# Top-k attention with two expert layers: the scores' PSUM tile becomes two tiles with two copies, and the planner's table gets new numbers

## The chip, the cores and the metric

The kernel runs on one core of a Trainium2 chip. The core has five engines with a queue each: TensorE (PE, its weight loads shown as PEld), VectorE (DVE), ScalarE (ACT), GpSimd (POOL) and SyncE (SP, which here issues the DMAs). Every queue works in the order in which the program was written; an instruction that waits holds up all that stand behind it on its engine. The metric is the device time of the whole program in microseconds.

## What is computed

Four batches of 576 tokens with 8 heads of 64 columns go through attention in which each query keeps its 32 largest scores, then through a dense layer pair, then through eight experts of 288 tokens each, which a greedy rule assigns.

```python
scores = scale * np.matmul(q, k.transpose(0, 1, 3, 2))
kth = np.partition(scores, -top_k, axis=-1)[..., -top_k:-top_k + 1]
scores = np.where(scores >= kth, scores, -1000000000.0)
attn = np.exp(scores - np.max(scores, axis=-1, keepdims=True))
attn = attn / (np.sum(attn, axis=-1, keepdims=True) + 1e-09)
x = np.matmul(attn, v)                       # then tokens x (heads * 64)
h = x @ w_in
g = np.where(h >= 1, h, np.where(h <= -1, 0.0, (h + 1) ** 2 / 4))
x = g @ w_out
logits = x @ w_gate                          # greedy: best (token, expert) pairs first,
# each token once, each expert at most 288 tokens
h = np.maximum(x[mask] @ w1[e], 0.0)
out[mask] = h @ w2[e]
```

## The kernel before

There are two phases, and the order of the instructions in each is made by a small planner inside the program. Every operation is recorded (`_Recorder`, L213) with an estimated cost, and `Program.issue` (L166) lays the operations out with a list scheduler. Whenever an engine is free, it takes the ready operation with the smallest key. An operation is ready when its inputs are done and a hand-over time has passed (`_delay`, L128, from the tables `LAT`, `TO` and `SELF`, L57 to L59, with a factor `LATX` of 1.5 in the first phase). The keys come first from ranks that the code sets, and then from a pass that runs backward. Of eleven such rounds in the first phase (`ROUNDS`, L44) and twenty-one in the second the one with the earliest planned end is issued. The planner knows of an order between two operations only where one writes what the other reads or writes (L107). The framework that builds the program adds the semaphores to the instructions in the order that the planner gives.

The first phase does attention in steps. A step is one batch, one block of 128 query tokens (the fifth block has 64) and one pair of heads: 64 full steps with two heads one after the other, and 16 short ones. `scores` (L497) makes the two halves of a head's 576 scores as two groups of matmuls, in two banks of one PSUM tile `pS` (L287): half 0 in bank 0, half 1 in bank 1. ScalarE copies both halves with one instruction to an SBUF tile `s` (L527). Then VectorE makes the fold (L531): the larger of half 0, read from bank 0, and half 1, read from the copy, to a tile `f`; for some heads VectorE also makes the smaller of the two (L533), and for the others GpSimd derives it. `topk` (L544) runs four maxima of eight and three replacements on VectorE, a mask on ScalarE and GpSimd, and the exponential on ScalarE. `transposed` and `values` transpose the weights through PSUM (`pPT`, `pQ`) and multiply with v. When 256 tokens are complete, `ffn_block` (L694) runs the dense pair on them through the banks `pH` and `pX`, split in high and low parts (`gh`, `gl`, `whi`, `wl`). TensorE fills its time between the attention steps with this. In the first 140 us VectorE also decodes the 32 pieces of 64-bit weights (`decode`, L415; first operation `pH<-stage` or `pH<-s`, L426).

The second phase (`second_phase`, L843) finishes the last dense block, routes the tokens to one expert after the other (small VectorE operations with short matmuls between them, into `pQ`, `pPT` and `pS`), gathers each expert's 288 rows with indirect DMAs from GpSimd (L1245), runs the expert, and scatters its rows. Beside that, `look` (L1212) reads weight pieces again and ScalarE sums them (`size`); from all sums `totals` (L1221) makes a flag, which all engines read at the end (L1381) before a branch that is not taken here.

The lines that decide the order around the scores:

```python
pS = psum.tile([128, 2, 512], F32, name="pS")
T.matmul(pS[:, hf, o_:o_ + n], q_t[:, z, k, :], ks[k][:, c0:c0 + n], ...)
A.activation(s_sb[:, i, :].rearrange("p (a x) -> p a x", a=2), pS[:, :, :288], AF.Relu)
V.tensor_tensor(out=f[i][:, :HW], in0=pS[:, 0, :HW], in1=s_sb[:, i, HW:], op=ALU.max)
```

Of the kernel before, what the change touches and what calls it, by code (L numbers as in the profile page):

```python
# [9 lines left out]
F32 = mybir.dt.float32  # L10
# [38 lines left out]
LOW_ACT, CLIP_ACT, R_UK = (), (0,) * 9, {}  # L49


class Program:
# [26 lines left out]
    def _new(self, eng):  # L79
        op = {"eng": eng, "calls": [], "cost": 0.0, "lat": self.LAT[eng], "deps": set(), "rank": self.rank,  # L80
              "n": len(self.ops)}
        self.ops.append(op)
        return op

    @staticmethod
    def _span(ap):
# [16 lines left out]
        if t.space == bass.MemoryType.PSUM:  # L103
            return t.name, 0, 128, lo * size // 2048 * 2048, (hi * size // 2048 + 1) * 2048
        return t.name, p0, p1, lo * size, (hi + 1) * size

    def add(self, eng, call, cost, reads, writes, lat=None):  # L107
        op = self.grp or self._new(eng)
        op["calls"].append(call)
# [18 lines left out]
    def _delay(self, a, b):  # L128
        e, f = a["eng"], b["eng"]
        if e == "sync":  # L130
            return a["lat"]
        return self.SELF[e] if e == f else a["lat"] * self.latx + self.TO.get((e, f), 0)

    def _pass(self, key, heads, tails, clock):
# [7 lines left out]
        free = dict.fromkeys(engs, 0.0)  # L142
        soon = {e: [] for e in engs}
# [4 lines left out]
        while len(order) < len(ops):  # L148
# [9 lines left out]
            stop[n] = free[e] = t + (clock.run(t, cost) if clock and e == "tensor" else cost)  # L158
# [7 lines left out]
    def issue(self, rounds=0):  # L166
# [10 lines left out]
        for r in range(rounds + 1):  # L177
            stop, order, end = self._pass(key, heads, tails, _Clock(self.warm))
            if best is None or end < best[0]:
                best = end, order  # L180
            if r < rounds:
                back = self._pass([-x for x in stop], tails, heads, None)
                key = [-x for x in back[0]]
        for n in best[1]:
            for call in ops[n]["calls"]:
                call()
        self.ops, self.hist = [], {}

# [24 lines left out]
class _Recorder:  # L213
# [5 lines left out]
    def __getattr__(self, method):  # L219
        def rec(*args, **kw):  # L220
# [12 lines left out]
            lat = None  # L233
            if eng == "vector":
# [3 lines left out]
                if method == "tensor_scalar" and not inp:  # L238
# [12 lines left out]
            elif eng == "gpsimd":  # L251
                cost = 148 + 2.1 * n
# [3 lines left out]
            elif method == "transpose":  # L256
                cost = 109
            else:
                f32 = args[1].dtype == F32
                if args[1].dtype == F32R:  # L260
                    cost = 10 + 0.43 * n
                else:
                    cost = 2 * max(107, n * 2 / 2.4) + 1 if f32 else max(25 if _free(args[1]) == 128 else 45, n / 2.4 + 3)
                if f32 and args[1].shape[-1] <= 64:
                    cost *= 0.63
            fn = getattr(getattr(P.nc, eng), method)
            P.add(eng, lambda: fn(*args, **kw), cost, reads, writes, lat)  # L267
# [11 lines left out]
def kernel(ctx: ExitStack, tc: tile.TileContext, qm, qt, kT, vm, vt,  # L279
# [7 lines left out]
    pS = psum.tile([128, 2, 512], F32, name="pS")  # L287
# [84 lines left out]
    def first_phase(exact, actx):  # L372
# [124 lines left out]
        def scores(b, j, p, r, exact):  # L497
# [19 lines left out]
            for i in range(2 if full else 1):  # L517
                for hf in range(2):
# [3 lines left out]
                    with P.group():  # L522
                        for x, (k, o_, c0, n) in enumerate(parts):
                            for z in range(2):
                                T.matmul(pS[:, hf, o_:o_ + n], q_t[:, z, k, :], ks[k][:, c0:c0 + n],
                                         start=(x + z == 0), stop=(x == len(parts) - 1 and z == 1))
                A.activation(s_sb[:, i, :].rearrange("p (a x) -> p a x", a=2), pS[:, :, :288],  # L527
                             AF.Copy if exact else AF.Relu)
                if not exact:
                    f.append(t_f())  # L530
                    V.tensor_tensor(out=f[i][:, :HW], in0=pS[:, 0, :HW], in1=s_sb[:, i, HW:], op=ALU.max)  # L531
                    if fold_dve(b, j, p, i):
                        V.tensor_tensor(out=f[i][:, HW:], in0=pS[:, 0, :HW], in1=s_sb[:, i, HW:], op=ALU.min)  # L533
# [123 lines left out]
        def values(b, j, ps, r, made):  # L657
# [3 lines left out]
            accs = [pQ[:, 256 + 128 * n:384 + 128 * n] for n in range(2)]  # L661
# [155 lines left out]
        for b in range(B):  # L817
            for j in range(5):
                for p in range(NP):
# [3 lines left out]
                    values(b, j, (p,), at, made)  # L823
                    made = []
                    at += 1.0 if j < 4 else 0.6
                    if j == 4 and b + 1 < B:
                        P.rank = at + R_K
                        load_pair(b + 1, p)
                    if p == NP - 1 and (b, j) == (B - 1, 4):
# [3 lines left out]
                        ffn_end(k, [pS[:, t] for t in range(2)])  # L833
# [6 lines left out]
        P.issue(0 if exact else ROUNDS)  # L840


    def second_phase(exact, rctx):  # L843
# [55 lines left out]
        XT0 = [pH[0], pH[1], pS[:, 0, :], pX[0]]  # L899
# [555 lines left out]
```

## Time and profile before

| what | value |
|---|---|
| median of three runs | 1122.76 us (1122.61 to 1126.74) |
| the profiled execution, its own time | 1125.48 us |
| its span | 1123.7 us |
| TensorE busy in the span | 1043.9 us (93%) |
| VectorE busy | 913.1 us (81%) |
| ScalarE busy | 808.3 us (72%) |
| GpSimd busy | 699.4 us (62%) |
| granted TensorE clock, mean | 0.957 |

The span runs from the first to the last instruction of the profiled execution; 1.8 us of its own time lie outside. Busy time is the time in which an engine had at least one instruction under way. A matmul's end is modelled, and matmuls overlap, so a TensorE that is busy all the time may still lose some time between instructions. A line of a wait says which engine and tile waited, for which engine and tile, how long in total and how often. All recorded operations carry the line of the recorder, L267, so they are told apart by their tiles.

### The profile page before, as it was taken

Reading aid. Unit: us, or ns where it says so; the run is one execution under the profiler, and the core shown is the slowest. Engines: PE = TensorE matmul, PEld = TensorE weight load, DVE = VectorE, ACT = ScalarE, POOL = GpSimd, SP = SyncE. Lnnn points to the kernel's source line nnn. Section 1 sums busy time; section 2 is a strip of 40 time slices with the busy share of each in tenths; the row PEclk is TensorE's granted clock in tenths of the full one; section 3 lists DMA queues with packets and bytes.
Section 4 is the critical chain, followed back from the end, with each engine's and each line's share of the span. In section 5 each row is a group of like instructions: output and inputs, shape, how many; then the busy total and the mean of one; then the engine's idle time right before and its main releaser. Section 6 shows DMA issues by size and latency. Waiting matters only on the chain.

```text
span 1123.7 us, 24286 instructions
## 1 busy us (share of the span) xinstructions
PE 1043.9 (93%) x8376; PEld 940.6 (84%) x8376; DVE 913.1 (81%) x2638; ACT 808.3 (72%) x1899; POOL 699.4 (62%) x880
## 2 busy tenths in 40 slices
PE   2687799999999999999999999999998999999995
PEld 1566589888888888899988889898976999999994
DVE  7899999899999889988989999994248998775530
ACT  4677787888898888877888988875314666666652
POOL 6997988987887888757689788773211143223111
PEclk9966689999999999999999999999988999999998
DMA  9743432351221342221234221212227777787721
GB/s 260 234 146 122 146 129 79 111 160 58 85 77 62 97 151 93 72 92 65 81 100 134 90 76 51 85 60 65 97 74 234 265 273 237 236 262 253 264 97 44
DMA packets 65783, 149.35 MB, mean 133 GB/s; under 512 B 15472, under 2 KB 23920, under 8 KB 65648
## 3 DMA queue, kind: packets, MB, share of 16 engines
q1 hardware_dynamic: 62576, 138.25, 37.7%
q0 software_dynamic: 3072, 9.44, 2.6%
q8 instruction: 68, 1.11, 0.4%
q14 instruction: 67, 0.55, 0.2%
HBM read 133.50 MB, written 14.16 MB: 131 GB/s over the span
## 4 chain that ended last, share of the span: by engine, by line
PE 64%; DVE 14%; ACT 7%; issue 5%; POOL 4%; DMA 4%; SPq 0%; POOLq 0%; DVEq 0%; ACTq 0%
PE pH L267 23%; PE pX L267 23%; PE pQ L267 7%; PE pS L267 7%; DVE f L267 5%; DVE m L267 5%; PE pPT L267 4%; ACT s L267 3%; DVE stage L267 2%; POOL s L267 2%; POOL XB L267 1%; ACT f L267 1%; DMA s<-in_w_in_dram 1%; DVE pH L267 1%; POOL f L267 1%
## 5 line engine op out<-in xcount | busy, mean ns | idle before, releaser
L267 PE MATMUL pH<-XB,W 128*128 128x256 f32 (+1 forms) x2496 | 360.1, 291 | 0.8 <-DVE L L267 0.5
L267 PEld LDWEIGHTS pH<-XB,W 128*128 128x128 f32 x2496 | 327.8, 190 | 8.2 <-issue 2.7
L267 DVE MAX8 m<-f 128x8 f32<-128x288 f32 (+1 forms) x576 | 290.9, 525 | 6.7 <-POOL f L267 1.1
L267 POOL TENSOR_TENSOR s<-s,f 128x576 f32<-128x576 f32 x144 | 204.2, 1432 | 29.5 <-ACT f L267 28.4
L267 DVE MATCH_REPLACE8 f<-m,f 128x288 f32<-128x288 f32 x432 | 190.2, 442 | 0.2
L267 PE MATMUL pX<-W,XB 128*128 128x512 f32 x608 | 184.9, 412 | 0.0
L267 PE MATMUL pS<-XB 128*128 128x288 f32 (+2 forms) x672 | 143.0, 324 | 37.8 <-DVE f L267 16.0
L267 POOL TENSOR_TENSOR XB<-stage,XB 128x512 fp32r<-128x512 f32 (+1 forms) x96 | 127.3, 1326 | 62.4 <-ACT XB L267 47.6
L267 PEld LDWEIGHTS pS<-XB 128*128 128x128 f32 x672 | 106.3, 201 | 57.8 <-DVE f L267 20.0
L267 ACT ACTIVATE s<-s,sm 128x576 f32<-128x576 f32 x144 | 111.8, 777 | 22.1 <-POOL s L267 21.5
L267 PEld LDWEIGHTS pX<-W,XB 128*128 128x128 f32 x608 | 108.2, 192 | 18.0 <-issue 2.4
L267 PE MATMUL pX<-XB,W 128*128 128x288 f32 x768 | 113.7, 299 | 0.0
L267 ACT ACTIVATE s<-pS 128x576 f32<-128x576 f32 x144 | 92.9, 645 | 25.7 <-PE pS L267 23.8
L267 ACT ACTIVATE f<-s,t_all 128x576 f32<-128x576 f32 x144 | 107.9, 772 | 2.9
L267 DVE TENSOR_TENSOR f<-pS,s 128x288 f32<-128x288 f32 x198 | 85.7, 448 | 23.3 <-ACT s L267 10.5
L267 PEld LDWEIGHTS pX<-XB,W 128*128 128x128 f32 x768 | 104.4, 188 | 0.0
L1245 POOL DMA_INDIRECT xg<-dram_x,idx x24 | 34.0, 1417 | 113.0 <-DVE idx L267 55.3
L267 PE MATMUL pPT<-ident,s 128*128 128x128 f32 x576 | 92.9, 286 | 7.0 <-ACT s L267 6.9
L1339 POOL DMA_INDIRECT out_dram<-yo,idx x24 | 28.3, 1179 | 110.3 <-ACT yo L267 107.9
L267 ACT ACTIVATE s<-pPT 128x512 f32<-128x512 f32 x144 | 85.2, 592 | 9.6 <-PE pPT L267 9.2
L267 DVE TENSOR_TENSOR W<-raw,W 128x1024 fp32r<-128x1024 f32 x64 | 77.1, 1219 | 15.7 <-ACT W L267 15.7
L267 PE MATMUL pQ<-s,v 128*64 128x128 f32 (+1 forms) x1280 | 87.2, 282 | 2.3 <-ACT tr L267 2.3
(206 smaller groups left out, 1906.6 us busy)
## 6 DMA issues: line engine op xcount, KB each, us to landing
wl<-dram_wlo SPq DMA_DIRECT2D x64, 512.0 KB, 3.3
raw<-in_w_dram SPq DMA_DIRECT2D x64, 512.0 KB, 5.5
s<-in_w_in_dram SPq DMA_DIRECT2D x18, 512.0 KB, 4.4
s<-in_w_out_dram SPq DMA_DIRECT2D x18, 512.0 KB, 3.9
qr<-in_qm_dram SPq DMA_DIRECT2D x128, 64.0 KB, 2.2
stage<-in_w_in_dram SPq DMA_DIRECT2D x14, 512.0 KB, 4.1
stage<-in_w_out_dram SPq DMA_DIRECT2D x14, 512.0 KB, 3.3
stage<-in_kT_dram SPq DMA_DIRECT2D x48, 144.0 KB, 2.8
```

The source lines that it names most:

```text
L267: P.add(eng, lambda: fn(*args, **kw), cost, reads, writes, lat)
L1245: return nc.gpsimd.indirect_dma_start(out=xg[:, g, :], out_offset=None, in_=x2d[:, :], in_offset=bass.IndirectOffsetOnAxis(ap=idx[:, g:g + ...
L1339: st = nc.gpsimd.indirect_dma_start(out=out, out_offset=bass.IndirectOffsetOnAxis(ap=idx[:, g:g + 1], axis=0), in_=yo, in_offset=None)
```

## The change

The tile `pS` of two banks becomes two tiles of one bank, `pS[0]` and `pS[1]`. In `scores` the group of half 1 comes first, and after each group ScalarE copies that half alone, so a head has two copies of 128x288 in place of one of 128x576. The folds are as before; they read bank 0 and the copy of half 1.

The planner's numbers change. A hand-over now has its own number for each pair of engines, and the factor of 1.5 is no longer used. A change of the kind of matmul (plain, 64-column, transpose) has a price (`TURN`). Six costs are altered: VectorE's scalar operations that write PSUM, GpSimd's long operations, and four kinds of matmul. PSUM tiles are now taken as wholes by the planner, which is the same for tiles of one bank. A search over shaken keys (`SEEDS`) and a grouping of steps (`PAIRS`) are added and left at values that do nothing: no seeds, and one step at a time.

```diff
-    LAT = {"vector": 140, "scalar": 170, "gpsimd": 75, "tensor": 200, "sync": 0}
-    TO = {("tensor", "vector"): 90, ("scalar", "tensor"): 100, ("gpsimd", "tensor"): 100, ("vector", "tensor"): 60}
-    SELF = {"vector": 128, "gpsimd": 103, "scalar": 0, "tensor": 0}
+    LAT = {"vector": {"scalar": 112, "gpsimd": 160, "tensor": 137, "vector": 128, "sync": 210},
+           "scalar": {"vector": 142, "gpsimd": 187, "tensor": 165, "scalar": 130, "sync": 255},
+           "gpsimd": {"vector": 170, "scalar": 102, "tensor": 117, "gpsimd": 130, "sync": 112},
+           "tensor": {"vector": 205, "scalar": 200, "gpsimd": 205, "tensor": 0, "sync": 300}}
+    TURN = {(0, 1): 90, (2, 1): 93, (1, 0): 150, (1, 2): 150, (2, 0): -81}
...
-        return self.SELF[e] if e == f else a["lat"] * self.latx + self.TO.get((e, f), 0)
+        return a["lat"] if e == "sync" else self.LAT[e][f]
...
-                if method == "tensor_scalar" and not inp:
+                if method == "tensor_scalar" and not inp and not outp:
                     cost = 69 + 0.52 * n
...
-                cost = 148 + 2.1 * n
+                cost = 148 + 2.1 * n + (27 if n > 500 else 0)
...
-    pS = psum.tile([128, 2, 512], F32, name="pS")
+    pS = [psum.tile([128, 512], F32, name=f"pS{i}") for i in range(2)]
...
-                for hf in range(2):
+                for hf in (1, 0):
...
-                                T.matmul(pS[:, hf, o_:o_ + n], q_t[:, z, k, :], ks[k][:, c0:c0 + n],
+                                T.matmul(pS[hf][:, o_:o_ + n], q_t[:, z, k, :], ks[k][:, c0:c0 + n],
...
-                A.activation(s_sb[:, i, :].rearrange("p (a x) -> p a x", a=2), pS[:, :, :288],
-                             AF.Copy if exact else AF.Relu)
+                    A.activation(s_sb[:, i, HW * hf:HW * hf + HW], pS[hf][:, :HW], AF.Copy if exact else AF.Relu)
...
-                    V.tensor_tensor(out=f[i][:, :HW], in0=pS[:, 0, :HW], in1=s_sb[:, i, HW:], op=ALU.max)
+                    V.tensor_tensor(out=f[i][:, :HW], in0=pS[0][:, :HW], in1=s_sb[:, i, HW:], op=ALU.max)
...
-        P.issue(0 if exact else ROUNDS)
+        P.issue(0, ()) if exact else P.issue(ROUNDS, SEEDS)
```

What the change does to the order is seen in the queues. The first place is ScalarE in the middle of the first phase, at the 85th and 86th of the 144 heads; `pS` is the tile of two banks, `s` the copy, and in brackets stands whose semaphores the instruction waits for. Before:

```order
L267 ACTIVATE s_107<-pS 128x576 [waits PE_49]
L267 ACTIVATE f_132<-sm_136 128x128 [waits DVE_49]
L267 ACTIVATE stage<-stage,mhalf 128x512 [waits DVE_49]
L267 ACTIVATE s_105<-pPT 128x512 [waits PE_49]
L267 ACTIVATE s_107<-pS 128x576 [waits PE_49]
```

After, where `pS_67` is bank 1 and `pS_66` is bank 0:

```order
L304 ACTIVATE s_108<-pS_67 128x288 [waits PE_49]
L304 ACTIVATE s_108<-pS_66 128x288 [waits PE_49]
L304 ACTIVATE stage<-stage,mhalf 128x512 [waits DVE_49]
L304 ACTIVATE f_133<-sm_137 128x128 [waits DVE_49]
L304 ACTIVATE s_108<-pS_67 128x288 [waits PE_49]
L304 ACTIVATE s_106<-pPT 128x512 [waits PE_49]
L304 ACTIVATE t_all<-m_139 128x2 [waits DVE_49]
L304 ACTIVATE s_108<-pS_66 128x288 [waits DVE_49]
```

Each copy became two, the copy of bank 1 ahead of that of bank 0, and the second head's copies are apart, with other work between them; its copy of bank 0 waits for VectorE, which before no score copy here did. In the whole program 47 of the 144 copies of bank 0 wait for a fold, and of the 198 folds 81 wait for the copy of bank 0 and 39 for that of bank 1; the others wait for neither by themselves.

The second place is TensorE's queue at the first expert's gathered rows `xg`; `ident` is the identity for transposes, `I_0` belongs to the ranks of the tokens, `W`, `XB` with `pX` to the last dense block. Before:

```order
L267 LDWEIGHTS I_0_9487
L267 MATMUL pQ<-C_9477,I_0_9487 128x8
L267 LDWEIGHTS ones_f
L267 MATMUL pPT<-ge_9489,ones_f 128x8 [waits DVE_49]
L267 MATMUL pH_69<-ident,xg_9524 128x96 [waits DMASW0_49]
L267 MATMUL pH_69<-ident,xg_9524 128x96 [waits DMASW1_49]
```

After:

```order
L304 LDWEIGHTS I_0_9632
L304 MATMUL pQ<-C_9622,I_0_9632 128x8
L304 MATMUL pX_73<-W_96,XB 128x512 x4
L304 MATMUL pX_73<-W_97,XB 128x512
L304 LDWEIGHTS ones_f
L304 MATMUL pPT<-ge_9633,ones_f 128x8 [waits DVE_49]
L304 MATMUL pX_73<-W_97,XB 128x512 x3
L304 MATMUL pX_73<-W_98,XB 128x512 x4
L304 MATMUL pX_73<-W_99,XB 128x512 x4
L304 MATMUL pH_70<-ident,xg_9669 128x96 [waits DMASW0_49]
```

Twelve `pX` matmuls of the last dense block now stand behind the ranks and ahead of the transposes of `xg`, where none stood. Counted from the router's last matmul that the gather needs (`Bt`, `oh`), 23 matmuls into `pX` stand ahead of the transposes, where 15 stood.

The third place is the end of ScalarE's queue. `s` is the last expert's result on its way, `yo` its rows before they are scattered, `size` belongs to the look at the weights, and `TENSOR_LOAD flag` is the reading of the flag. Before:

```order
L267 ACTIVATE s_107<-pX_71 128x288 [waits PE_49]
L267 ACTIVATE size_9533,sizes<-s_106 128x512 [waits DMAHW6_49,Activation_49]
L267 ACTIVATE size_9533,sizes<-size_9533 128x512 [waits Activation_49]
L267 ACTIVATE s_107<-pX_72 128x288 [waits PE_49]
L267 ACTIVATE yo_9528<-pS 96x512 [waits DMASW2_49,PE_49]
L267 ACTIVATE yo_9526<-pX_71 96x512 [waits DMASW3_49,PE_49]
L267 ACTIVATE yo_9527<-pS 96x512 [waits DMASW4_49,PE_49]
L1381 TENSOR_LOAD flag [waits DVE_49]
```

After:

```order
L304 ACTIVATE size_9678,sizes<-size_9678 128x512 [waits Activation_49]
L304 ACTIVATE s_108<-pX_73 128x288 [waits PE_49]
L304 ACTIVATE yo_9673<-pS_66 96x512 [waits DMASW2_49,PE_49]
L304 ACTIVATE yo_9671<-pX_72 96x512 [waits DMASW3_49,PE_49]
L304 ACTIVATE yo_9672<-pS_66 96x512 [waits DMASW4_49,PE_49]
L304 ACTIVATE size_9678,sizes<-s_107 128x512 [waits DMAHW6_49,Activation_49]
L304 ACTIVATE size_9678,sizes<-size_9678 128x512 [waits Activation_49]
L1421 TENSOR_LOAD flag [waits DVE_49]
```

The last pair of `size` operations has moved behind the three `yo` copies, and with it the small operations on VectorE and TensorE that make the flag.

## Rows read from the trace of the kernel before

**Rows 1.** Busy time of the engines by stretch of the span (us).

```profile
core 0: us, PE busy (x) PEld busy (x) DVE busy (x) ACT busy (x) POOL busy (x), PEclk, DMA share, GB/s
0.00:28.00 28.00, 5.88 (x22) 4.84 (x23) 21.06 (x46) 11.25 (x19) 17.49 (x26) 1.00 0.95 260
28.00:140.00 112.00, 84.54 (x458) 67.09 (x456) 103.72 (x284) 81.09 (x196) 100.68 (x119) 0.71 0.49 163
140.00:756.00 616.00, 604.83 (x4931) 540.67 (x4932) 568.94 (x1716) 522.29 (x1281) 493.59 (x640) 0.99 0.28 91
...
868.00:1107.00 239.00, 238.68 (x2127) 233.93 (x2127) 160.53 (x403) 153.15 (x326) 57.88 (x64) 1.00 0.68 229
```

**Rows 2.** Groups by form, whole span: busy us, mean ns; idle before, its releasers.

```profile
L267 PE MATMUL pS<-XB 128*128 128x288 f32 x608 | 137.5, 331 | 37.8 <-DVE f L267 16.0 <-POOL XB L267 15.8 <-ACT s L267 3.3
...
L267 ACT ACTIVATE s<-pS 128x576 f32<-128x576 f32 x144 | 92.9, 645 | 25.7 <-PE pS L267 23.8 <-POOL f L267 1.0 <-POOL XB L267 0.2
...
L267 ACT ACTIVATE s<-pX 128x288 f32<-128x288 f32 x32 | 13.1, 408 | 28.5 <-PE pX L267 28.4
...
L267 DVE TENSOR_TENSOR f<-pS,s 128x288 f32<-128x288 f32 x198 | 85.7, 448 | 23.3 <-ACT s L267 10.5 <-PE pS L267 6.1 <-PE pQ L267 2.0
```

**Rows 3.** Waits, 140 to 756 us: who <- for whom: total us, times, longest.

```profile
PEld pS L267 <- DVE f L267: 7.3, 13, 1.2
PE pS L267 <- DVE f L267: 6.3, 11, 0.8
...
DVE f L267 <- ACT s L267: 8.9, 11, 1.6
...
ACT s L267 <- PE pS L267: 16.6, 24, 2.3
```

**Rows 4.** Waits of TensorE for the folds from 0 to 140 us.

```profile
PE pS L267 <- DVE f L267: 9.7, 8, 2.1
```

**Rows 5.** Timeline of score steps, ACT, PE, DVE: start, length, operation, [wait <- releaser].

```profile
402.47 0.63 ACT L267 ACTIVATE s<-pS 128x576 f32<-128x576 f32 x1
...
403.00 0.27 ACT L267 ACTIVATE s<-pQ 128x128 f32<-128x128 f32 x1
...
405.60 0.51 PE L267 MATMUL pS<-XB 128*128 128x288 f32 x2
...
406.35 0.63 ACT L267 ACTIVATE s<-pS 128x576 f32<-128x576 f32 x1
...
408.03 0.45 DVE L267 TENSOR_TENSOR f<-pS,s 128x288 f32<-128x288 f32 x1
...
408.62 0.51 PE L267 MATMUL pS<-XB 128*128 128x288 f32 x2 [0.84 <-DVE f L267]
```

**Rows 6.** Timeline of the first gather: TensorE, then GpSimd, then TensorE.

```profile
851.13 1.41 PE L267 MATMUL pX<-W,XB 128*128 128x512 f32 x5
...
854.93 0.71 PE L267 MATMUL pX<-W,XB 128*128 128x512 f32 x2
...
853.33 1.23 POOL L1245 DMA_INDIRECT xg<-dram_x,idx  x1 [28.17 <-DMA s<-in_w_in_dram]
...
859.74 0.55 PE L267 MATMUL pH<-ident,xg 96*128 96x96 f32 x2 [0.96 <-DMA xg<-dram_x,idx]
```

**Rows 7.** The tail: timelines of ACT and DVE, then the chain on POOL.

```profile
1104.93 0.65 ACT L267 ACTIVATE size<-s 128x512 f32<-128x512 f32 x1
...
1109.96 0.59 ACT L267 ACTIVATE yo<-pS 96x512 f32<-96x512 f32 x1 [0.25 <-PE pS L267]
...
1106.46 0.18 DVE L267 TENSOR_SCALAR sizes<-sizes 128x32 f32<-128x32 f32 x1 [0.57 <-ACT size L267]
...
1108.31 0.14 DVE L267 TENSOR_REDUCE flag<-flags 1x1 int32<-1x3 f32 x1
...
1111.65 0.03 POOLq L1381
...
1111.95 0.92 POOL out_dram L1339
```

More of the change, by code (lines that the diff above doesn't have):

```diff
@@ L103, in _span, with add @@
         if t.space == bass.MemoryType.PSUM:
-            return t.name, 0, 128, lo * size // 2048 * 2048, (hi * size // 2048 + 1) * 2048
+            return t.name, 0, 128, 0, 1 << 30
         return t.name, p0, p1, lo * size, (hi + 1) * size
-    def add(self, eng, call, cost, reads, writes, lat=None):
+    def add(self, eng, call, cost, reads, writes, lat=None, mode=0):
         op = self.grp or self._new(eng)
+        op["mode"] = mode
         op["calls"].append(call)
@@ L142, in _pass @@
         free = dict.fromkeys(engs, 0.0)
+        mode = 0
         soon = {e: [] for e in engs}
@@ L157, in _pass @@
             cost = ops[n]["cost"]
-            stop[n] = free[e] = t + (clock.run(t, cost) if clock and e == "tensor" else cost)
+            if clock and e == "tensor":
+                cost += self.TURN.get((mode, ops[n]["mode"]), 0)
+                mode = ops[n]["mode"]
+                cost = clock.run(t, cost)
+            stop[n] = free[e] = t + cost
             for m, gap in tails[n]:
@@ L176, in issue, with look @@
         key, best = [o["rank"] for o in ops], None
-        for r in range(rounds + 1):
+        def look(key):
+            nonlocal best
             stop, order, end = self._pass(key, heads, tails, _Clock(self.warm))
             if best is None or end < best[0]:
-                best = end, order
+                best = end, order, key
+            return stop
+        for r in range(rounds + 1):
+            stop = look(key)
             if r < rounds:
@@ L183, in issue @@
                 key = [-x for x in back[0]]
+        for seed in seeds:
+            look(_shaken(best[2], best[0], seed))
         for n in best[1]:
@@ L187, in issue, with _shaken, draw @@
         self.ops, self.hist = [], {}
+def _shaken(key, end, seed):
+    x = (seed * 2654435761 + 12345) % 4294967296
+    def draw():
+        nonlocal x
+        x = (x * 1664525 + 1013904223) % 4294967296
+        return x / 2147483648.0 - 1.0
+    size = SHAKE * 2.0 ** -(seed % 5)
+    if seed % 2 == 0:
+        return [k + size * draw() for k in key]
+    at = 0.5 * end * (draw() - 1.0)
+    return [k + 2.0 * size * draw() if abs(k - at) < 40000.0 else k for k in key]
 class _Clock:
@@ L237, in rec @@
                     cost += 64
-                if method == "tensor_scalar" and not inp:
+                outp = any(a.tensor.space == bass.MemoryType.PSUM for a in writes if hasattr(a.tensor, "space"))
+                if method == "tensor_scalar" and not inp and not outp:
                     cost = 69 + 0.52 * n
@@ L251, in rec @@
             elif eng == "gpsimd":
-                cost = 148 + 2.1 * n
+                cost = 148 + 2.1 * n + (27 if n > 500 else 0)
+                if n == S and writes[0].dtype == F32R:
+                    cost += 115
             elif eng == "sync":
@@ L660, in values @@
             w = 128 if full else 64
-            accs = [pQ[:, 256 + 128 * n:384 + 128 * n] for n in range(2)]
+            accs = [pQ[:, 256 + 128 * (x % 2):384 + 128 * (x % 2)] for x in ps]
             with P.group():
@@ L822, in first_phase @@
                     made.append(transposed(b, j, p, at, s_sb, rinv, wide))
-                    values(b, j, (p,), at, made)
-                    made = []
+                    done = len(made) == PAIRS
+                    if done:
+                        ps = tuple(range(p + 1 - PAIRS, p + 1))
+                        values(b, j, ps, at, made)
+                        made = []
                     at += 1.0 if j < 4 else 0.6
-                    if j == 4 and b + 1 < B:
+                    if done and j == 4 and b + 1 < B:
                         P.rank = at + R_K
-                        load_pair(b + 1, p)
+                        for x in ps:
+                            load_pair(b + 1, x)
                     if p == NP - 1 and (b, j) == (B - 1, 4):
@@ L832, in first_phase @@
                         k, P.rank = late.pop()
-                        ffn_end(k, [pS[:, t] for t in range(2)])
+                        ffn_end(k, pS)
                     if p == NP - 1:
@@ L1172, in route @@
             V.tensor_tensor_scan(sc, tk, tk, 0.0, op0=ALU.add, op1=ALU.bypass)
-            T.matmul(pS[:, 1, 8:9], tri, sc[:, NT - 1:NT], start=True, stop=True)
+            T.matmul(pS[1][:, 8:9], tri, sc[:, NT - 1:NT], start=True, stop=True)
             pos = rt([128, NT], F32, "pos")
-            V.scalar_tensor_tensor(out=pos, in0=sc, scalar=pS[:, 1, 8:9], in1=most, op0=ALU.add, op1=ALU.min)
+            V.scalar_tensor_tensor(out=pos, in0=sc, scalar=pS[1][:, 8:9], in1=most, op0=ALU.add, op1=ALU.min)
             places(ph, ei, pos)
```

39 lines of the change are left out of this document (21 added, 18 removed).

## The prediction

> **What bounds the kernel now.** I read the busy times by stretch first [rows 1]. The program has different limits in different stretches. Up to 28 us the DMA engines are busy 95% of the time and TensorE only 5.88 us. From 28 to 140 us VectorE is the limit: it is busy 103.72 of 112 us, because it decodes weights beside the top-k, while TensorE has 84.54 us of work at a mean granted clock of 0.71. From 140 to 756 us TensorE is the limit, with 604.83 of 616 us and a clock of 0.99, so only 11.2 us can be gained there by keeping it fed; VectorE has 47.1 us free, ScalarE 93.7 us. From 868 to 1107 us TensorE is busy 238.68 of 239 us, and no order of the other engines can shorten that. So the change can act in the first 140 us, in the 11.2 us, at the start of the experts, and at the end.
>
> Then I read what ends TensorE's waits in the middle [rows 3]. It waits for a fold before it may overwrite `pS`: 6.3 us in 11 waits, and its weight load, which stands just ahead of the matmul, 7.3 us in 13. ScalarE waits 16.6 us for TensorE's scores. The first two rows are the same stalls seen twice, so I count 6.3 us, over half of the 11.2. In the first 140 us the same wait costs 9.7 us in 8 cases [rows 4]. The timeline of a case [rows 5]: a copy runs from 406.35 for 0.63 us and is done at 406.98, but the fold starts only at 408.03, since VectorE has other work first; the next scores' matmuls wait 0.84 us for it and start at 408.62. The copy held nothing up there; the fold was late by itself.
>
> **Part 1, two copies in place of one.** A copy of 128x576 lasts 645 ns, one of 128x288 (from another PSUM tile) 408 ns [rows 2]. So 144 x (2 x 408 - 645) ns = 24.6 us more ScalarE time, at most; at the pace at which the next instruction starts, 0.53 us after the large copy [rows 5], it is less. All of it lies on ScalarE, which has 93.7 us free in the middle. Queued behind a longer copy are the weights' exponentials and the copies of `pPT`, for which TensorE waits. I take 0, with 3 us as the upper end: 24.6 x 11.2 / 93.7, as if the extra time reached TensorE in the proportion in which it has idle time left.
>
> **Part 2, what the halves release.** Now the half in bank 1 comes first and needs only its own copy to be overwritten; the half in bank 0 still waits for the fold. In a wait as in [rows 5] TensorE can do the bank-1 pair meanwhile: two matmuls take 0.51 us end to end and one lasts 0.331 [rows 2], so they follow each other by 0.18, and a pair is worth 0.36 us of a wait. With 11 waits that is 4.0 us. Bank 1's copy also starts a pair earlier and is 0.24 us shorter, so the fold's second source is there 0.6 us sooner; that helps 11 waits of VectorE worth 8.9 us [rows 3], but VectorE has time to spare here, so I give it, and the planner's numbers (hand-overs per pair of engines without the 1.5 factor), only 1 us more. Middle: **-5 us**, between 0 and -11.2.
>
> **Part 3, a wait that the code does not show.** In the changed order 81 of the 198 folds wait for the copy of bank 0, which they do not use, and 47 of the 144 copies of bank 0 wait for a fold: both read bank 0, and they are kept from doing it together. In the kernel before, one copy stood ahead of the fold anyway. The planner does not know of this order. The Trainium skill has the reason ("PSUM — Partial Sum Buffer", section "PSUM bank collisions raise a hardware error"): two different engines that access one bank and partition quadrant at the same time, two readers included, raise an error, so software must order them. By that rule the two copies cannot free the fold from bank 0's copy, so the 1 us that Part 2 gives the earlier fold goes, and the middle is -4.0 instead of -5, the sum 1116.7 instead of 1115.7; no row of the trace before shows two readers of one bank together, so it neither agrees nor differs. The price from rows: a fold held for a whole copy loses 0.408 us [rows 2], so 81 of them lose at most 33 us of VectorE time; a copy held for a fold loses at most 0.448, 47 of them 21 us of ScalarE time. Both fit in the 47.1 and 93.7 us free in the middle, and most folds will find the copy finished, as in [rows 5] where the fold came 1.05 us after it. I take 0 and keep a loss as a rival.
>
> **Part 4, the first 140 us.** Three things move: the first two loads are now those of k instead of a weight piece (first decode perhaps 1 us later, first scores earlier), the first seven folds stand up to thirteen places further ahead in VectorE's queue, and the costs of the decode are now planned near their real size. The 9.7 us of waits [rows 4] is what could go, worth 8 x 0.36 = 2.9 us by the reckoning of Part 2. VectorE has 8.3 us free between 28 and 140 us, which limits the rest. On the other side about a dozen of the first 24 folds (VectorE's first 300 instructions, of 330 in this stretch [rows 1]) wait for ScalarE: 12 x 0.408 = 4.9 us where VectorE is the limit. I take **-2 us**, between -8 and +5.
>
> **Part 5, the first gather.** In the changed order 23 matmuls of the last dense block stand between the router's last matmul for the gather and the expert's first transposes, where 15 stood. In the trace GpSimd starts the gather at 853.33, TensorE ends its `pX` work at 855.64 and starts the transposes at 859.74 [rows 6]. Eight more matmuls at (1.41 - 0.71) / 3 = 0.23 us each fill 1.9 us of that hole: **-1.9 us**, between 0 and -2.5.
>
> **Part 6, the end.** The last pair of `size` operations starts at 1104.93 [rows 7], inside time that nothing waits for. It now comes behind the last `yo` copy, which starts at 1109.96 and lasts 0.59. From the first `size` to the end of the flag's last operation (1108.31 + 0.14) it took 3.52 us, part of it while TensorE was still in its last `pX` work, which is then over; I take 2.9. From 1110.5, where the last `yo` copy lets ScalarE go on, the flag comes at 1113.4. GpSimd, the last engine to read it, did so at 1111.65. So **+1.8 us**, between 0 (if the last scatter, 1111.95 to 1112.87, decides the end instead) and +2.4.
>
> The second phase between these places keeps its work: 0, within 2 either way.
>
> **The sum** against the profiled execution's own 1125.48 us: 0 - 5 + 0 - 2 - 1.9 + 1.8 = -7.1, so 1118.4. That execution was 2.7 us above the median; I put the same -7.1 on the median 1122.76: **1115.7 us**, or -0.63%. A measurement of this kernel can tell about 0.5%, 5.6 us, from no change: faster means below 1117.1, slower above 1128.4.
>
> **Rivals.** *Nothing measurable.* The fold is late through VectorE's own queue, as [rows 5] says, and the fold still holds bank 0; then only the 4.0 us of Part 2 are real or less, the first 140 us give nothing, and Part 6 takes 1.8 back: 1122.8 - 4.0 - 1.9 + 1.8 + 0 = 1118.7, and up to 1125 where the new order loses as much as it gains elsewhere; I put it at 1121. For it speaks that only 11.2 us are to be had; against it that the waits are the largest of TensorE's in the middle. In this case the change would do what its code says and not what it is worth, since fold and copy of bank 0 are still in sequence.
>
> *Slower by Part 3.* The place is the fold in VectorE's queue. Each fold that waits for the bank-0 copy also holds up the maxima behind it, then the mask, the transposes and TensorE. Up to 33 us would use VectorE's 47.1 us; it decides once the waits in a stretch are larger than VectorE's spare time there, and it is worst before 140 us where only 8.3 are spare. If a quarter of 33 reaches TensorE, that is +8.3 and nothing of Parts 2 and 4 is left: 1122.8 + 8.3 - 1.9 + 1.8 = 1131. For it speaks that the planner prices none of this; against it that VectorE's wait for the copy was so far only 8.9 us, and would be shortened.
>
> *More than forecast, in the first 140 us.* TensorE idles 27.5 us between 28 and 140 us [rows 1]. If the plan with truer numbers takes half of it, 13.7 us instead of 2, the time is 1104. Against it: VectorE is busy 93% there, and its work stays.
>
> **How the numbers follow.** Forecast 0.50 (1108 to 1120, of which 0.37 below 1117.1), nothing measurable 0.25, slower 0.17, more than forecast 0.08. So faster 0.45, same 0.13 + 0.25 = 0.38, slower 0.17. The range 1104 to 1130 leaves out some 0.04 below and 0.11 above, and covers the bounds of the terms.
>
> **What would show it.** Right: between 140 and 756 us TensorE's waits of `pS` for the fold fall from 6.3 to about 2 us, and its busy share rises; the gap ahead of the first expert's transposes shrinks by 2 us; the flag is read near 1113 us less the gain. Wrong: a row in which the fold waits for the copy by tens of us with TensorE's idle time up (the slower rival); or a middle that lasts as long as before with the same waits under another name; or a stretch up to 140 us that grows because VectorE waits there.

## The result

The changed kernel takes 1132.3 us (median of 12), the kernel before 1125.62 us beside it. The ratio is 1.0072, 95% interval 1.006 to 1.0083 (the two medians alone give 1.0059): slower by 0.72%, against a forecast of 1115.7 us, 0.63% faster, and a range up to 1130. The profiled execution took 1135.01 us and its span is 1133.0 us, 9.3 us longer than the span of before. That is more than the 6.7 us between the medians, because this execution lies 2.7 us above its own median; what follows accounts for the 9.3 us of the two traces.

The stretches of [rows 1] in the changed kernel (columns as there):

```profile
core 0: us, PE busy (x) PEld busy (x) DVE busy (x) ACT busy (x) POOL busy (x), PEclk, DMA share, GB/s
0.00:28.00 28.00, 5.77 (x19) 4.07 (x19) 18.95 (x43) 11.19 (x20) 18.70 (x27) 1.00 0.91 260
28.00:140.00 112.00, 85.34 (x474) 69.49 (x474) 104.78 (x290) 84.83 (x225) 101.16 (x120) 0.74 0.51 163
140.00:756.00 616.00, 607.27 (x4920) 542.25 (x4921) 565.15 (x1716) 520.03 (x1395) 492.74 (x639) 0.99 0.29 91
...
868.00:1107.00 239.00, 234.85 (x2076) 229.83 (x2075) 162.26 (x410) 151.16 (x319) 58.22 (x64) 0.99 0.69 223
```

TensorE has the same 8376 matmuls. In the three first stretches it is busy 5.77, 85.34 and 607.27 us, where it was 5.88, 84.54 and 604.83; the table below has the changed kernel ahead at the end of them, by 0.2 us. From 868 to 1107 us it is busy 234.85 us where it was 238.68, with 2076 matmuls where 2127 were. Of the waits of [rows 3], TensorE's for the fold fell and VectorE's for the copy rose (middle of the first phase; total, times, longest):

```profile
PE pS L304 <- DVE f L304: 2.4, 7, 0.7
...
DVE f L304 <- ACT s L304: 11.3, 22, 2.1
```

In the same stretch TensorE's waits for ScalarE's copies rose. Before, then after:

```profile
PE pPT L267 <- ACT s L267: 0.8, 2, 0.6
```

```profile
PE pS L304 <- ACT s L304: 1.9, 3, 1.2
PE pPT L304 <- ACT s L304: 1.1, 3, 0.5
```

Windows of equal length don't say when the same work is done. So I gave each matmul in its order the usual distance to the next one of its kind, from the trace of before, and read at which time a given sum is reached. That is a reckoning from the traces, not a view of the profile. In the first row are the times of before; below it, how much later (+) or earlier (-) the same amount of work is reached, and by how much the span differs; the kernels e1 to e12 are those of the next section. With three other choices of the usual distance (other percentiles, kinds without their tiles) the first column moves by up to 6.6 us, the next three by up to 2.3 and the last two by up to 1.1; so the first column bears no reading of a few us.

| kernel | 40 us of work | 430 | 550 | 640 | 730 | 850 | span |
|---|---|---|---|---|---|---|---|
| before, at | 138.8 | 621.1 | 766.9 | 875.9 | 969.1 | 1092.2 | 1123.7 |
| changed | -2.7 | -1.2 | -0.2 | -2.0 | +4.5 | +5.2 | +9.3 |
| e1 | -8.8 | -9.1 | -3.2 | -3.9 | -3.8 | -3.6 | -5.6 |
| e2 | +0.5 | -0.7 | +3.8 | +2.9 | +9.2 | +9.0 | +12.0 |
| e3 | -2.7 | -2.2 | -1.2 | -1.5 | -1.8 | -0.8 | -0.7 |
| e4 | +0.2 | -0.1 | +0.9 | -1.6 | -0.4 | -0.2 | +3.2 |
| e5 | -5.6 | -8.5 | -6.4 | -9.5 | -9.8 | -9.1 | -11.4 |
| e6 | -3.7 | -6.7 | -2.4 | -5.6 | -5.6 | -5.0 | -7.3 |
| e7 | -0.6 | -0.7 | -0.6 | -0.7 | +7.8 | +7.7 | +10.3 |
| e8 | -9.1 | -9.7 | -3.8 | -2.6 | -1.7 | -2.2 | -4.2 |
| e9 | +0.9 | -0.3 | +0.6 | -0.4 | +0.5 | +1.1 | +1.1 |
| e10 | -1.9 | +4.8 | +7.2 | +6.5 | +6.3 | +6.6 | +4.4 |
| e11 | -2.5 | -7.9 | -3.1 | -4.3 | -4.6 | -4.6 | -6.8 |
| e12 | +0.5 | -10.3 | -9.8 | -11.2 | -11.4 | -8.2 | -10.4 |

The changed kernel is 2.0 us ahead when the experts begin, 5.2 us behind once they run, and loses another 4.1 us at the very end. The first of these losses lies between 876 and 1001 us. Before, in the windows of it (the granted clock is the third number from the end):

```profile
868.00:890.00 22.00, 22.00 (x216) 20.98 (x216) 19.81 (x40) 14.62 (x28) 3.61 (x3) 1.00 0.86 298
890.00:910.00 20.00, 20.00 (x197) 19.32 (x196) 19.14 (x58) 14.93 (x30) 5.96 (x6) 1.00 0.75 257
...
930.00:950.00 20.00, 20.00 (x197) 19.40 (x196) 17.83 (x59) 12.56 (x28) 4.09 (x5) 1.00 0.71 236
...
990.00:1010.00 20.00, 19.68 (x178) 18.89 (x177) 16.03 (x52) 12.39 (x26) 3.21 (x5) 1.00 0.82 257
```

After:

```profile
868.00:890.00 22.00, 20.25 (x201) 19.28 (x200) 18.75 (x48) 13.19 (x27) 4.55 (x3) 0.97 0.63 203
890.00:910.00 20.00, 20.00 (x190) 19.31 (x190) 17.12 (x53) 13.32 (x29) 3.98 (x3) 0.95 0.67 220
...
930.00:950.00 20.00, 18.56 (x171) 17.66 (x171) 13.80 (x40) 9.96 (x21) 2.59 (x4) 0.91 0.81 260
...
990.00:1010.00 20.00, 19.03 (x184) 18.22 (x182) 13.60 (x27) 10.15 (x21) 2.47 (x3) 1.00 0.87 279
```

TensorE's busy time is short by 1.75, 1.44 and 0.97 us in three windows, against 0.32 before: 3.8 us more idle time. Behind the pauses the granted clock is below full, that is, 1.2 GHz for part of the window: 22 x 0.03 + 20 x 0.05 + 20 x 0.09 = 3.5 us of time lost. Together 7.3 us, and the table has 7.2 (from -2.0 to +5.2). The timeline shows what TensorE waited for (start, length, operation, wait):

```profile
856.27 1.58 PE L304 MATMUL pH<-ident,xg 96*128 96x96 f32 x6 [1.23 <-DMA xg<-dram_x,idx]
...
886.83 0.30 PE L304 MATMUL pH<-ident,xg 96*128 96x96 f32 x1 [1.57 <-DMA xg<-dram_x,idx]
...
937.95 1.46 PE L304 MATMUL pH<-XB,W 128*128 128x288 f32 x9 [1.44 <-DVE XB L304]
...
1002.13 1.05 PE L304 MATMUL pH<-XB,W 128*128 128x288 f32 x6 [0.86 <-DVE XB L304]
```

The line of the DMA issues on the gathers (count, median us from issue to landing):

```profile
xg<-dram_x,idx POOLq DMA_INDIRECT x24, 7.3
```

At 886.83 it stands at the transposes of the second expert's rows and they have not landed; at 937.95 and 1002.13 VectorE is late with `XB`, which the traces so far do not tie to a gather. The end, in a timeline:

```profile
1115.24 0.59 ACT L304 ACTIVATE yo<-pS 96x512 f32<-96x512 f32 x1 [0.25 <-PE pS L304]
...
1115.74 0.64 ACT L304 ACTIVATE size<-s 128x512 f32<-128x512 f32 x1
...
1117.24 0.92 POOL L1379 DMA_INDIRECT out_dram<-yo,idx  x1 [0.22 <-ACT size L304]
...
1118.52 0.14 DVE L304 TENSOR_REDUCE flag<-flags 1x1 int32<-1x3 f32 x1
```

The last copy of `yo` starts at 1115.24 and the last pair of `size` after it, as the order said; the flag is done at 1118.66, 0.5 us behind the end of GpSimd's last scatter instruction.

### The profile page after: what moved, and what is told of

It reads as the page before. It is cut to its first block, busy times and chain, and to the rows that moved or that the text cites. A ratio compares the mean times of both kernels' runs of the same rounds, so it can differ in the third digit from the quotient of the medians.

```text
span 1133.0 us, 24417 instructions
## 1 busy us (share of the span) xinstructions
PE 1050.9 (93%) x8376; PEld 946.9 (84%) x8376; DVE 908.7 (80%) x2638; ACT 810.6 (72%) x2043; POOL 701.3 (62%) x880
## 4 chain that ended last, share of the span: by engine, by line
PE 61%; DVE 15%; ACT 8%; POOL 7%; DMA 4%; issue 3%; SPq 0%; POOLq 0%; DVEq 0%; ACTq 0%
PE pX L304 22%; PE pH L304 22%; PE pQ L304 8%; PE pS L304 6%; DVE f L304 5%; ACT s L304 4%; DVE m L304 4%; PE pPT L304 4%; POOL XB L304 2%; POOL f L304 2%; DMA raw<-in_w_dram 1%; POOL s L304 1%; DVE stage L304 1%; ACT XB L304 1%; DMA xg<-dram_x,idx 1%
## 5 line engine op out<-in xcount | busy, mean ns | idle before, releaser
L304 PE MATMUL pH<-XB,W 128*128 128x256 f32 (+1 forms) x2496 | 365.3, 292 | 2.5 <-DVE XB L304 2.3
L304 PE MATMUL pS<-XB 128*128 128x288 f32 (+2 forms) x672 | 148.1, 325 | 27.8 <-ACT XB L304 15.7
L304 PEld LDWEIGHTS pS<-XB 128*128 128x128 f32 x672 | 109.3, 202 | 46.1 <-POOL W L304 15.6
L304 ACT ACTIVATE s<-pS 128x288 f32<-128x288 f32 x288 | 113.6, 410 | 33.0 <-PE pS L304 19.7
L304 DVE TENSOR_TENSOR f<-pS,s 128x288 f32<-128x288 f32 x198 | 87.2, 450 | 23.3 <-ACT s L304 13.9
L1285 POOL DMA_INDIRECT xg<-dram_x,idx x24 | 37.0, 1544 | 100.1 <-DVE idx L304 50.7
L304 ACT ACTIVATE W<-raw 128x1024 fp32r<-128x1024 f32 x64 | 66.3, 1056 | 37.5 <-DMA raw<-in_w_dram 34.9
```

The lines of the kernel that those rows point to most:

```text
L1285: return nc.gpsimd.indirect_dma_start(out=xg[:, g, :], out_offset=None, in_=x2d[:, :], in_offset=bass.IndirectOffsetOnAxis(ap=idx[:, g:g + ...
```

## The experiments

Theory A: the two copies are not the loss; the planner's new numbers are, in the second phase. Theory B, the rival on record: two copies of which the fold may not read bank 0 together. Each run is compared with the kernel before on the same chip.

**e1_split.** The kernel before with the two tiles and copies alone; all of the planner's numbers are as before.

```diff
+    pS = [psum.tile([128, 512], F32, name=f"pS{i}") for i in range(2)]
+                for hf in (1, 0):
+                    A.activation(s_sb[:, i, HW * hf:HW * hf + HW], pS[hf][:, :HW], ...)
```

> The kernel before with the two tiles, the two copies and the order of halves, and all the planner's old numbers; its second phase stands in the order of before. Theory A (the loss of 9.3 us comes from the new numbers in the second phase, between 868 and 1000 us and at the end): within 0.3% of before, the time after 868 us as before. Theory B (two copies and folds that may not read bank 0 together are the loss): slower by 0.5 to 0.8%, with VectorE waiting for copies between 140 and 756 us.

Ratio 0.9947 (0.9928 to 0.9967). Theory B falls: the copies are a gain, which neither theory had expected. The stretch of the first phase that VectorE limits:

```profile
28.00:140.00 112.00, 86.16 (x505) 69.87 (x504) 109.31 (x299) 89.06 (x236) 106.20 (x127) 0.77 0.51 165
```

TensorE's wait for the fold from 0 to 140 us:

```profile
PE pS L267 <- DVE f L267: 2.5, 5, 0.7
```

The wait of [rows 4] fell from 9.7 us to 2.5, VectorE is busy 109.31 of 112 us where it had 103.72, and the first 40 us of TensorE's work are done 8.8 us earlier (5.7 to 12.8 by the other choices). The granted clock of the stretch is 0.77 in place of 0.71 as well; how much of the lead comes from fewer waits and how much from the clock is not shown. About 6 us of the lead go between 612 and 655 us:

```profile
630.00:636.00 6.00, 5.14 (x33) 4.48 (x34) 5.95 (x20) 5.53 (x18) 1.83 (x6) 0.87 0.19 66
636.00:642.00 6.00, 6.00 (x40) 5.60 (x40) 3.81 (x15) 4.64 (x13) 3.86 (x5) 0.56 0.07 22
642.00:648.00 6.00, 6.00 (x57) 5.79 (x55) 5.37 (x17) 5.21 (x15) 4.87 (x9) 1.00 0.10 25
```

TensorE has 0.86 us of pauses in the first window, and in the second the clock is at 0.56 with the engine busy throughout. This shows where they went. It is not one execution alone: e8, which has the same first phase, loses its lead in the same column of the table (-9.7 to -3.8).

**e2_numbers.** The changed kernel with one tile and one copy, so the new numbers alone (the copy is that of 128x576 again, and the planner takes the two banks of the tile apart, as before).

```diff
-    pS = [psum.tile([128, 512], F32, name=f"pS{i}") for i in range(2)]
+    pS = psum.tile([128, 2, 512], F32, name="pS")
```

> The changed kernel's planner numbers with one tile and one copy as before; its second phase stands in the order of the changed kernel. Theory A: slower than before by 0.5 to 0.9%, 6 to 8 us lost between 868 and 1000 us and 3 to 5 us at the end. Theory B: within 0.3% of before.

1.0119 (1.0091 to 1.0146): slower by more than the whole change, and more than expected. Numbers and copies add up: 1.0119 x 0.9947 = 1.0065, where the change has 1.0072.

**e3_old_second.** The change, with the old numbers in the second phase. The cut shows the hand-overs; the old costs, and no price of turns, come back there too.

```diff
+        if self.warm and e != "sync":
+            return self.SELF[e] if e == f else a["lat"] + self.TO.get((e, f), 0)
         return a["lat"] if e == "sync" else self.LAT[e][f]
```

> The changed kernel with the old numbers in the second phase alone, which then stands in the order of before. Theory A: at most as slow as before, ratio 0.995 to 1.001, the loss after 868 us gone. Theory B: still slower by 0.5 to 0.8%.

1.0017 (0.9997 to 1.0038), just outside the range of theory A, and TensorE is busy again while the experts run:

```profile
868.00:1107.00 239.00, 237.64 (x2125) 233.12 (x2124) 158.99 (x399) 152.35 (x325) 55.45 (x64) 1.00 0.67 225
```

So the new numbers cost 0.55% in the second phase (1.0072 against 1.0017). But e1 and e3 have the same second phase and the same copies, and differ by 0.7%: the new numbers cost about as much in the first phase. Theory A has only half of the loss.

**e4_gather_lag.** Of the second phase's numbers one stood out. Before, an operation's own time behind it counted (`a["lat"] * self.latx`); in the change only SyncE's does. The code gives 3000 ns behind a gather; the planner now took 117 ns.

```diff
-        return a["lat"] if e == "sync" else self.LAT[e][f]
+        return a["lat"] if e == "sync" or a["lat"] else self.LAT[e][f]
```

> The changed kernel, in which the planner again adds the 3000 ns between a gather and its readers and the 2000 ns behind a scatter that the code gives (with the new table it takes 117 ns for GpSimd to TensorE instead). Theory A1 (this lost number is the cause in the second phase): TensorE's wait of 1.6 us for the gathered rows at 887 us and the clock's fall after it go, 4 to 7 of the 7.2 us come back, ratio to before 1.001 to 1.004 with the late flag left. Theory A2 (another of the new numbers): ratio 1.005 to 1.009 as the changed kernel.

1.0032 (1.0015 to 1.005), as theory A1 expected. Most of the loss between 876 and 1001 us is gone (-1.6 to -0.2 us in the table, where the change went from -2.0 to +5.2):

```profile
868.00:1107.00 239.00, 237.58 (x2122) 233.12 (x2121) 159.89 (x401) 153.16 (x325) 54.21 (x64) 1.00 0.69 227
```

The two pauses for `XB` are gone with the one for the gathered rows, and the clock stays at 1.00; so they go with the same lost number, by a way that I did not follow.

**e7_no_gather_lag.** The reverse: the kernel before without these times.

```diff
-    P.add("gpsimd", partial(gather, g), 1500, [...], [xg[:, g, :]], 3000)
+    P.add("gpsimd", partial(gather, g), 1500, [...], [xg[:, g, :]])
-    P.add("gpsimd", partial(scatter, g, yo), 1100, [...], [spacer], 2000)
+    P.add("gpsimd", partial(scatter, g, yo), 1100, [...], [spacer])
```

> The kernel before with one thing changed: the planner no longer gets the 3000 ns behind a gather and the 2000 ns behind a scatter, and takes GpSimd's usual hand-over. First phase as before. Theory A1 (this is what the second phase lost): slower by 3 to 6 us, ratio 1.003 to 1.006, with TensorE waiting for gathered rows and the clock falling after it. Otherwise: 0.999 to 1.001.

1.0074 (1.0048 to 1.01), more than expected. From -0.7 us at 876 us it goes to +7.8 at 977 us, and TensorE's pauses are the gathers (timeline; in brackets the wait):

```profile
859.30 0.74 PE L267 MATMUL pH<-ident,xg 96*128 96x96 f32 x2 [1.88 <-DMA xg<-dram_x,idx]
...
889.51 0.30 PE L267 MATMUL pH<-ident,xg 96*128 96x96 f32 x1 [0.87 <-DMA xg<-dram_x,idx]
891.19 0.30 PE L267 MATMUL pH<-ident,xg 96*128 96x96 f32 x1 [1.38 <-DMA xg<-dram_x,idx]
...
922.49 0.30 PE L267 MATMUL pH<-ident,xg 96*128 96x96 f32 x1 [1.48 <-DMA xg<-dram_x,idx]
923.30 0.30 PE L267 MATMUL pH<-ident,xg 96*128 96x96 f32 x1 [0.50 <-DMA xg<-dram_x,idx]
```

Between 868 and 1010 us TensorE idles 4.56 us in this kernel, where it was 0.32, and the granted clock is 0.86 from 910 to 930 us and 0.97 from 930 to 950 us, 3.4 us of time more. A further 2.6 us are lost at the end (+7.7 to +10.3 in the table), where the flag is done only after the last scatter has started.

So the lost time behind gather and scatter alone is enough for a loss of this size, and giving it back takes most of it away. How much is the gather's and how much the scatter's part I did not separate; all waits shown are for gathered rows.

**e5_wide_lags.** The first phase's loss: the old hand-overs were times 1.5 there, the new ones are not.

```diff
-        return a["lat"] if e == "sync" else self.LAT[e][f]
+        return a["lat"] if e == "sync" else self.LAT[e][f] * self.latx
```

This and the four that follow have the old second phase, as e3 has.

> Two tiles and two copies, the old numbers in the second phase (as e3_old_second), and in the first phase the new table with its hand-overs again times 1.5, as the old ones were; new costs and turns stay. The first load is again a weight piece. Theory C (the hand-overs without the margin lose the gain of the two copies in the first 140 us): ratio to before 0.993 to 0.997, as e1_split. Theory D (the altered costs lose it): 1.000 to 1.003, as e3_old_second.

0.9926 (0.9898 to 0.9953): just below the range of theory C. **e6_new_costs** has the old hand-overs, with their 1.5, and only the new costs and turns:

```diff
-        if self.warm and e != "sync":
+        if e != "sync":
+            return self.SELF[e] if e == f else a["lat"] * self.latx + self.TO.get((e, f), 0)
```

> As e3_old_second, but with the old hand-overs in the first phase too; only the altered costs and the price of turns remain of the new numbers, and only in the first phase. Theory C: 0.993 to 0.997. Theory D: 1.000 to 1.003.

0.9932 (0.9908 to 0.9955). The costs are harmless, and so are the new hand-overs once they have the margin. **e10_split_no_margin** takes the margin from e1:

```diff
-LATX, LATR, GRP = 1.5, 1.0, 1
+LATX, LATR, GRP = 1.0, 1.0, 1
```

> The kernel of e1_split (0.9947) with the factor on the old hand-overs of the first phase 1.0 instead of 1.5, nothing else. Theory C (the margin on the hand-overs is what keeps the gain of the two copies): 1.000 to 1.003, like e3_old_second, with TensorE's work of the first 140 us done 3 to 6 us later than in e1_split. Otherwise (the values of the new table, pair by pair, are the cause): 0.993 to 0.997.

1.0049 (1.0028 to 1.0069): 1% slower than e1, and more than expected. **e11_near** and **e12_more_margin** change the factor of e5 to 1.48 and to 2.0:

```diff
-LATX, LATR, GRP = 1.5, 1.0, 1
+LATX, LATR, GRP = 2.0, 1.0, 1
```

> The kernel of e5_wide_lags (0.9926) with a factor of 1.48 instead of 1.5: a change that means nothing by itself, but gives another order. If the plans behave alike: 0.990 to 0.995. If one order differs from the next by chance as much as the differences explained here: outside that, up to 1.000.

> The kernel of e5_wide_lags (0.9926) with a factor of 2.0 instead of 1.5. If more margin still helps: 0.987 to 0.991; if 1.5 is enough: 0.992 to 0.996; too much would show as idle time of TensorE between 140 and 756 us.

0.9906 (0.9871 to 0.9942) and 0.9874 (0.9853 to 0.9895). An order made from almost the same number gives the same time within the noise. That is one pair; e8 below, where only the order of the second phase differs from e1, is 0.25% above it, within the noise; the margin makes 0.9% (e3 to e5) and 1.0% (e10 to e1), found twice with different numbers. A factor of 2.0 has the lowest time of all, 1112.34 us, but its interval overlaps that of 1.48, so more than 1.5 is not clearly better. The middle of the first phase without margin (e10), then with 2.0 (e12):

```profile
140.00:756.00 616.00, 604.05 (x4870) 534.76 (x4871) 559.89 (x1692) 521.21 (x1385) 487.64 (x632) 0.99 0.28 90
```

```profile
140.00:756.00 616.00, 610.86 (x5015) 547.46 (x5015) 570.53 (x1744) 527.27 (x1419) 499.07 (x650) 1.00 0.28 92
```

TensorE idles 11.95 us there in the one and 5.1 in the other, and has 145 matmuls more done. Theory C had put the gain of the margin in the first 140 us. For e10 that is half of it: e10 is 6.9 us behind e1 at 40 us of work and 13.9 at 430, and for e12 it does not hold, since e12 is no earlier at 40 than the kernel before and gains 10 us by 430. And e3, e4 and e9 share the changed kernel's first phase, but reach the 40 us at -2.7 to +0.9: one trace doesn't settle 3 us there. One more thing goes with the margin: the first load is one of k in the changed kernel, e2, e3, e4, e9 and e10, and a weight piece in the kernel before and all the others. No run parts the two. But e10 loses as much again behind the first 140 us, and e12, with the weight piece first, is not ahead there, so the first load alone does not make these differences.

**e8_split_flag and e9_lag_flag** are about the end. Both let the planner see that something follows the flag:

```diff
             V.tensor_reduce(out=flag, in_=flags, axis=AX, op=ALU.max)
+            P.add("sync", lambda: None, 5000, [flag], [])
```

> The kernel of e1_split, where the planner also has a 5 us operation behind the flag, so that the last look at the weights comes ahead of the last copies of rows. If the late flag costs time at the end: 1 to 3 us less than e1_split (ratio to before 0.992 to 0.994). If the last scatter decides the end: as e1_split, 0.9947 within 0.001.

0.9972 (0.9951 to 0.9993), no gain, and outside both ranges. The run tells nothing on the end, because in e1 the flag (1104.93) already comes ahead of the last scatter. It only shows another order of the second phase, which gives back about 2 us of the lead between 550 and 730 us of work.

> The kernel of e4_gather_lag (ratio to before 1.0032), where the planner also has a 5 us operation behind the flag; the last pair of the look's sums now stands ahead of the last copies of rows, and the flag ahead of the last scatter. In the traces so far the span ends 8.4 to 10.9 us behind the last scatter where the flag came before it, and 13.3 to 14.3 us behind the flag where it came last. If that order is the cause: 3 to 5 us less than e4_gather_lag, ratio 0.9985 to 1.001, and at most 11 us behind the last scatter. If not: 1.002 to 1.004.

0.9999 (0.9974 to 1.0024), from 1.0032, as expected; the two intervals overlap, but in the traces e4 loses 3.4 us behind 850 us of work (-0.2 to +3.2) and e9 none. The flag and the last scatter in its timeline:

```profile
1109.46 0.14 DVE L304 TENSOR_REDUCE flag<-flags 1x1 int32<-1x3 f32 x1
...
1113.10 0.92 POOL L1380 DMA_INDIRECT out_dram<-yo,idx  x1 [0.22 <-issue]
```

What follows the last of flag and scatter (ends, us; the spans are those of the pages):

| kernel | flag | last scatter | span | behind the later one |
|---|---|---|---|---|
| before | 1108.45 | 1112.87 | 1123.7 | 10.8 |
| e1 | 1104.93 | 1109.35 | 1118.1 | 8.8 |
| e9 | 1109.60 | 1114.02 | 1124.8 | 10.8 |
| e12 | 1100.31 | 1104.73 | 1113.3 | 8.6 |
| changed | 1118.66 | 1118.16 | 1133.0 | 14.3 |
| e2 | 1122.42 | 1121.92 | 1135.7 | 13.3 |
| e4 | 1113.17 | 1112.66 | 1126.9 | 13.7 |
| e7 | 1120.17 | 1120.65 | 1134.0 | 13.4 |

In e7 the flag is done 0.44 us after the last scatter has started (1119.73), so it too is read late, and the span ends 13.8 us behind it. The kernels left out, all with the flag ahead of the last scatter, end 8.4 to 10.9 us behind that scatter.

## Why the prediction was wrong

**Part 1** held in its price and not quite in its value of 0: a small copy lasts 410 ns (page of the changed kernel: 113.6 us busy for 288), the forecast took 408, and ScalarE is busy 20.7 us longer with them. TensorE's waits for ScalarE's copies rose from 0.8 to 3.0 us in the middle, which is within the upper end of 3 us. Whether the longer copies or the new order make them is not parted.

**Part 2** was right in the wait that it names and wrong in what that is worth. TensorE's waits for the fold in the middle fell from 6.3 us to 2.4, as the part on what would show it said, but 2.2 of these 3.9 us came back as waits for copies, and the middle as a whole gave nothing: the lead is 2.7 us at 136 us and 0.2 at 767, and by none of the choices for the usual distance does it grow between them, where -5 was forecast. With the old numbers (e1) it is the same, 9.1 us at 612 and 3.2 at 764; there the gain is in the first 140 us, 8.8 us, where the reckoning of Part 2 had given 2.9. VectorE, the limit there, is busy 5.6 us longer in that stretch, and the clock is higher; which of them decides is not shown. The gain does not need the new numbers, to which I gave 1 us of gain. They cost 0.7%.

**Part 3** held in its value: the order between fold and copy exists, folds wait 22 times for copies in the middle instead of 11, for 11.3 us instead of 8.9; the row does not tell which of the two copies a fold waited for. No wait of TensorE shows these 2.4 us. By the rule of the Trainium skill ("PSUM — Partial Sum Buffer", section "PSUM bank collisions raise a hardware error") the two readers of bank 0 have to take turns. The semaphores here make them do so, and no run lets both read at once, so no trace here tests the rule. The slower rival, whose time (1131) is nearly that measured, is right by accident: with the same two copies and folds e1 is faster than before, so its mechanism does not make the loss.

**Part 4** and the middle forecast -7 us together. The changed kernel is 2.7 us ahead at 136 us, and 0.2 at 767. That the 2.7 is near the -2 of Part 4 is luck as far as can be told: e3, e4 and e9 have the same first phase and stand at -2.7, +0.2 and +0.9. The step that failed here is the one that gave "the planner's numbers (hand-overs per pair of engines without the 1.5 factor)" a gain, 1 us in Part 2: without the factor they cost 0.9% (e3 against e5), and the old ones without it 1.0% (e10 against e1). A likely reason is that without the margin the plan puts each reader right behind its writer, so that on engines that work in order any delay makes the queue wait. e5, e10, e11 and e12 show that the margin is worth 0.9 to 1.4%; that the delays of single instructions are the reason is argued, not shown.

**Part 5** held: the first transposes come at 856.27, not 859.74, and the lead grows by 1.8 us between 767 and 874 us, where 1.9 were forecast.

**Part 6** was right in its place and wrong in its size: the flag is done 1.4 us behind the start of the last scatter, where 1113.4 against 1111.95 was worked out, but it costs 4.1 us and not 1.8. I had taken the time behind the reading of the flag as fixed. Before, the span ended 12.0 us behind GpSimd's reading of it (done at 1111.68 by [rows 7]); now it ends 14.3 us behind the flag.

**The second phase, "0, within 2 either way",** is the step that turned the sign: +7.2 us. In the traces the sum is -0.2 by 767 us (Parts 1 to 4), -1.8 (Part 5), +7.2 and +4.1 (Part 6), together +9.3, where -7.1 was forecast. The line of the diff that does it was in front of me. `_delay` drops `a["lat"]` for all engines but SyncE, and the gathers and scatters are the only other operations that had been given a time of their own. The order also showed the gathered rows' transposes in another place; I read this only as a gain (Part 5). For the median of 7.3 us from a gather's issue to its landing, the planner had 4.6 us with the old numbers (1500 for the operation, 3000 behind it, 100 from GpSimd to TensorE) and 1.6 with the new.

## What to carry to other kernels

When a planner's table is replaced, list every operation that had a number of its own, and look whether the new code still reads it; a transfer that is planned as done too early can stall an in-order queue, and here half of the loss in that place was the clock that fell behind the pauses. Shorter hand-overs, one for each pair of engines, did not give a better static order here; with a factor of 1.5 or 2.0 on them the order was 0.9 to 1.4% faster. And run the parts of a mixed change apart: this one holds a gain of 0.5% and two losses, and with a margin of 2.0 and the old second phase (e12) it is 1.3% faster than the kernel before.

## What the runs showed of the hardware

The end of the program takes 8.4 to 10.9 us behind the last scatter where the flag is done before that scatter starts, and 13.3 to 14.3 us behind the flag where it is done later; why it takes 8.6 in some kernels and 10.8 in others stays open. In the changed kernel's second phase TensorE's pauses of 1.57 and 1.44 us were each followed by a granted clock below full (0.95 and 0.91 in the windows), the one of 0.86 us was not (1.00); the clock cost about as much as the pauses, 3.5 against 3.8 us. The 24 gathers of the changed kernel took 7.3 us (median) from issue to landing.
